# The first four steps of a fused Fourier and SoLU kernel: the next unit begun ahead of the last square, and the first sign's square ahead of the second sign's mean on ScalarE

## Chip, cores and metric

One core of a Trainium2 chip. The metric is the device time of one execution in microseconds (us). A timed value lies about 2.1 us above the span that the trace of the same execution shows, so times are compared with times and spans with spans. The experiments ran on three chips (1, 10 and 12), each kernel beside before on the same chip.

## The reference, cut to what matters

```python
def _attn_ref(x):                       # x: (8, 3136, 256)
    X = np.fft.fft(x, axis=1)
    X = np.fft.fft(X, axis=2)
    return X.real.astype(np.float32)

def _moe_ref(x, w_in, w_out, g_ln):     # x: (25088, 256), w_in: (256, 1024), w_out: (1024, 256)
    h = x @ w_in
    h_max = np.max(h, axis=-1, keepdims=True)
    e = np.exp(h - h_max)
    sm = e / (np.sum(e, axis=-1, keepdims=True) + 1e-09)
    solu = h * sm
    mu = np.mean(solu, axis=-1, keepdims=True)
    var = np.mean((solu - mu) ** 2, axis=-1, keepdims=True)
    ln = (solu - mu) / np.sqrt(var + 1e-06) * g_ln
    return (ln @ w_out).astype(np.float32)
```

## The kernel before

After a start phase that loads and narrows the weights and transforms the first pair of batches, the kernel works through 100 units of 128 rows, one unit in each step. A unit has two signs (rows k and mirrored rows), except that unit 0 has one. Names in the traces: xa and xb are loads of the next pair's input; zd is the first transform's result in DRAM, and g are its parts read back from there for the matmuls that make q; T is the table of these matmuls. A matmul of fp32 data leaves two records in the trace, a transpose one. The parts of a step that matter here:

```python
    def take2(t, ps):                       # q: second transform, PSUM to SBUF
        t.q = qpool.tile([P, KD * P], FP32, tag="q", name="q")
        nc.scalar.copy(t.q, ps)

    def spread(t):                          # r: one row of q becomes a column, 0.5 KB
        t.r = small.tile([P, 1], FP32, tag="r", name="r")
        nc.sync.dma_start(out=t.r, in_=t.q[0:1, P : 2 * P])

    def even(t, ps):                        # VectorE; waits for r
        ...
        nc.vector.scalar_tensor_tensor(out=t.ev, in0=w_mid, scalar=t.r, in1=ps, op0=ALU.mult, op1=ALU.add)

    # join: VectorE writes h = ev +- odd and its maximum; expo: ScalarE writes u = exp(h - max)

    def product(t, s, alone):               # VectorE: u = h * u and its sum; then the mean
        ...
        if alone:                           # steps 0 to 3
            nc.scalar.mul(out=t.nmean[:, s : s + 1], in_=t.usum[:, s : s + 1], mul=-1.0 / FF)
        else:
            nc.gpsimd.tensor_scalar(...)

    def square(t, s):                       # ScalarE, into h
        nc.scalar.activation(out=t.h[s], in_=t.u[s], func=ACT.Square, bias=t.nmean[:, s : s + 1],
                             accum_out=t.ssq[:, s : s + 1])

    # turn_whole (units 0 to 3): 16 TensorE transposes into four PSUM tiles ps_t, copied to uT,
    #   the first sign's two by ScalarE, the second's two by VectorE.
    #   All PSUM tiles of one bank (ps2 of q, ps_t, ps_o) share one pool of four.
    # down: 8 matmuls ps_o <- uT, Wo for each sign, four steps after the unit's own

        for i in range(len(units) + lag):   # lag = whole = 4
            ...
            if cur:
                cur.batch, cur.w = batch, i % 2
                even(cur, up(cur, 0))       # up: matmuls ps_h <- q, Wi
                odd = up(cur, 1)
            if nxt:                         # unit i + 2
                take2(nxt, transform2(pairs[nxt.p], nxt.k1))
                spread(nxt)
            if prv:
                turn_whole(prv)
            if cur:
                join(cur, odd)
            ...                             # copies ps_t to uT on VectorE
            if cur:
                expo(cur)
            ...                             # down of unit i - 4
            if cur:
                for s in cur.signs:
                    product(cur, s, i < whole)
                if i == 1:
                    weights.centre()        # VectorE: Wo = Wo - wbar, 128x2048
                for s in cur.signs:
                    square(cur, s)
                    if i >= whole:
                        turn_blocks(cur, s) # later units: blocks on VectorE, moved by DMA
            ...
            if i == 0:
                turn(first, 1, nc.sync)     # four g <- zd transfers
            ...
            if ahd:
                ahead(ahd, cur.k1)          # step 0: two xa and two xb loads of the next pair
```

Each engine runs its instructions in this program order.

## Time and profile before

| | before |
|---|---|
| time, first three runs | 1188.53, 1188.77, 1187.46 us |
| span of the profiled run (a fourth execution, timed at 1191.05 us) | 1188.9 us |
| busy share of TensorE, VectorE, ScalarE, GpSimd | 97, 76, 57, 41% |
| end of the start phase (ScalarE's copy w_mid begins) | 55.87 us |
| first ps_o, after which TensorE has no gap | 95.12 us |

### The profile page before, as it was taken

How to read it: one execution, taken by the hardware profiler on the slowest of the kernel's cores; microseconds unless marked ns; L12 is line 12 of the kernel's file. 1: busy time of each engine (PE TensorE's matmuls, PEld its weight loads, DVE VectorE, ACT ScalarE, POOL GpSimd, SP SyncE). 2: the span in 40 equal slices, each digit the busy share in tenths (PEclk: the TensorE clock that was granted, in tenths of full speed). 3: DMA queues.
4: the chain of work that ended last, by engine and by line, in shares of the span. 5: the costliest groups of instructions: out<-in, count | busy, mean ns of one | idle time of the engine just before them, and what ended most of it. 6: DMA issues, size and time to landing. Idle time of an engine off the chain costs nothing.

```text
span 1188.9 us, 15920 instructions
## 1 busy us (share of the span) xinstructions
PE 1154.8 (97%) x4720; PEld 875.7 (74%) x4720; DVE 905.3 (76%) x1234; ACT 679.6 (57%) x1411; POOL 493.0 (41%) x955
## 2 busy tenths in 40 slices
PE   2989999999999999999999999999999999999998
PEld 1556777778777777777777777777777777777787
DVE  7788777777778877787778878777786887877780
ACT  4566565656546656565555656565554555655561
POOL 3034445443545444433544453433453344333433
PEclk9999999999999999999999999999999999999999
DMA  9672877756775765654685775664684453544534
GB/s 239 191 188 47 197 180 178 202 142 156 178 170 155 189 172 153 171 145 134 166 187 158 182 177 152 159 179 121 151 200 128 112 150 98 147 111 120 142 91 118
DMA packets 458455, 185.39 MB, mean 156 GB/s; under 512 B 425751, under 2 KB 440351, under 8 KB 458369
## 3 DMA queue, kind: packets, MB, share of 16 engines
q1 hardware_dynamic: 444608, 146.22, 48.8%
q0 software_dynamic: 13760, 38.16, 11.8%
q8 instruction: 38, 0.62, 0.2%
q14 instruction: 49, 0.39, 0.1%
HBM read 44.78 MB, written 38.80 MB: 70 GB/s over the span
## 4 chain that ended last, share of the span: by engine, by line
PE 94%; DMA 2%; DVE 2%; ACT 1%; issue 1%; SPq 0%; DVEq 0%; ACTq 0%
PE ps_o L331 57%; PE ps_h L227 28%; PE ps L171 5%; PE ps L199 3%; DMA raw_in<-in_moe_w_in_dram 1%; PE wps L462 1%; DMA r<-q 1%; DVE u L259 0%; ACT h L271 0%; DVE y L123 0%; DVE h L241 0%; ACT u L251 0%; DVE xa L131 0%; DVE y L122 0%; SPq L367 0%
## 5 line engine op out<-in xcount | busy, mean ns | idle before, releaser
L331 PE MATMUL ps_o<-Wo,uT 128*128 128x256 f32 x3136 | 695.1, 380 | 0.0
L331 PEld LDWEIGHTS ps_o<-Wo,uT 128*128 128x128 f32 x3136 | 612.1, 196 | 63.0 <-issue 0.9
L227 PE MATMUL ps_h<-Wi,q 128*128 128x512 f32 x800 | 360.4, 593 | 1.7 <-DVE nmax L241 0.8
L259 DVE SCALAR_TENSOR_TENSOR u<-h,u 128x1024 f32<-128x1024 f32 x196 | 240.0, 1225 | 55.2 <-ACT u L251 28.4
L241 DVE CUSTOM_DVE_ANT_0 h<-ev,ps_h 128x1024 f32<-128x1024 f32 x196 | 231.7, 1219 | 50.5 <-PE ps_h L227 41.0
L227 PEld LDWEIGHTS ps_h<-Wi,q 128*128 128x128 f32 x800 | 151.5, 190 | 150.7 <-issue 142.3
L271 ACT ACTIVATE h<-u,nmean 128x1024 f32<-128x1024 f32 x196 | 225.0, 1149 | 55.4 <-POOL nmean L264 54.2
L264 POOL TENSOR_SCALAR nmean<-usum 128x1 f32<-128x1 f32 x189 | 76.6, 405 | 428.7 <-DVE u L259 428.3
L233 DVE SCALAR_TENSOR_TENSOR ev<-w_mid,r,ps_h 128x1024 f32<-128x1024 f32 x100 | 127.9, 1279 | 134.4 <-PE ps_h L227 124.2
L251 ACT ACTIVATE u<-h,neg 128x1024 f32<-128x1024 f32 x196 | 225.4, 1150 | 6.4
L299 DVE STREAM_TRANSPOSE v<-u 128x1024 f32<-128x1024 f32 x192 | 228.9, 1233 | 0.1
L205 ACT COPY q<-ps 128x256 f32<-128x256 f32 x100 | 37.0, 371 | 283.8 <-PE ps L199 247.6
L336 ACT ACTIVATE ot<-ps_o,rs 128x256 f32<-128x256 f32 x196 | 87.0, 461 | 60.9 <-PE ps_o L331 55.0
L343 POOL DMA_INDIRECT out_dram<-ot,idx x96 | 103.1, 1074 | 37.5 <-issue 22.8
L171 PE MATMUL ps<-y,F 98*100 98x258 f32 (+3 forms) x288 | 72.7, 390 | 23.4 <-DVE y L124 23.4
L199 PEld LDWEIGHTS ps<-T,g 128*128 128x128 f32 x400 | 60.1, 191 | 47.8 <-issue 45.9
L286 POOL TENSOR_TENSOR rs<-v,neg_half 128x2 f32<-128x2 f32 (+1 forms) x100 | 84.1, 841 | 7.8
L249 ACT ACTIVATE neg<-nmax 128x1 f32<-128x1 f32 x196 | 38.2, 195 | 62.6 <-DVE nmax L241 62.6
L283 POOL TENSOR_SCALAR v<-ssq 128x2 f32<-128x2 f32 (+1 forms) x100 | 23.7, 237 | 118.3 <-ACT h L271 118.3
L171 PEld LDWEIGHTS ps<-y,F 98*100 98x100 f32 x288 | 46.3, 180 | 35.7 <-DVE y L124 22.4
L199 PE MATMUL ps<-T,g 128*128 128x128 f32 x400 | 60.7, 275 | 0.1
L187 POOL DMA_DIRECT2D g<-zd x76 | 45.4, 610 | 30.1 <-DMA zd<-z_g 26.8
(73 smaller groups left out, 462.9 us busy)
## 6 DMA issues: line engine op xcount, KB each, us to landing
uT<-v SPq DMA_DIRECT2D x752, 128.0 KB
out_dram<-ot SPq DMA_DIRECT2D x100, 128.0 KB
g<-zd POOLq DMA_DIRECT2D x72, 160.0 KB, 5.3
xa<-in_x_dram SPq DMA_DIRECT2D x28, 392.0 KB
zd<-z SPq DMA_DIRECT2D x24, 400.0 KB
raw_in<-in_moe_w_in_dram SPq DMA_DIRECT2D x4, 512.0 KB
raw_out<-in_moe_w_out_dram SPq DMA_DIRECT2D x2, 1024.0 KB
r<-q SPq DMA_DIRECT2D x100, 0.5 KB
```

Source lines behind the costliest of these rows:

```text
L171: nc.tensor.matmul(o[..., cs], F[:, 2 * t + h, :], i[..., cs], start=first, stop=True, skip_group_check=True)
L199: nc.tensor.matmul(o, g[:, k, h * P : (h + 1) * P], table, start=(h == 0), stop=True, skip_group_check=True)
L227: nc.tensor.matmul(ps[:, fs], t.q[:, c * P : (c + 1) * P], Wi[:, c, fs], start=True, stop=True)
L233: nc.vector.scalar_tensor_tensor(out=t.ev, in0=w_mid, scalar=t.r, in1=ps, op0=ALU.mult, op1=ALU.add)
L241: nc.vector.tensor_tensor_reduce(out=t.h[s], in0=t.ev, in1=ps, scale=1.0, scalar=-3.0e38, op0=ALU.subtract if s else ALU.add, op1=ALU.max, ...
L251: nc.scalar.activation(out=t.u[s], in_=t.h[s], func=ACT.Exp, bias=t.neg[:, s : s + 1], accum_out=t.esum[:, s : s + 1])
L259: nc.vector.scalar_tensor_tensor(out=t.u[s], in0=t.h[s], scalar=1.0, in1=t.u[s], op0=ALU.mult, op1=ALU.mult, accum_out=t.usum[:, s : s + 1])
L271: nc.scalar.activation(out=t.h[s], in_=t.u[s], func=ACT.Square, bias=t.nmean[:, s : s + 1], accum_out=t.ssq[:, s : s + 1])
L299: nc.vector.transpose(out=t.batch.v[:, t.w, :, o], in_=t.u[s])
L331: nc.tensor.matmul(ps, uT[:, c, :, s], Wo[:, c, :], start=(c == 0), stop=(c == KF - 1))
L336: nc.scalar.mul(out=t.ot[s], in_=ps, mul=t.rs[:, s : s + 1])
L343: dma = nc.gpsimd.indirect_dma_start(out=out, out_offset=bass.IndirectOffsetOnAxis(ap=idx[:, i : i + 1], axis=0), in_=t.ot[s], in_offset=None)
```

## The change

The intent is to let ScalarE use its wait between the two means, and to have the next unit's q, and its transfer r, ready sooner in the first steps. The whole diff:

```diff
--- before.py
+++ after.py
@@ -604,28 +604,36 @@
         weights.load_table(1)
         lag = 4
         whole = 4
+
+        def begin(i):
+
+            cur = units[i]
+            if i % 2 == 0:
+                batches.append(Batch(i >= whole))
+            cur.batch, cur.w = batches[-1], i % 2
+            even(cur, up(cur, 0))
+            cur.odd = up(cur, 1)
+            if i + 2 < len(units):
+                nxt = units[i + 2]
+                take2(nxt, transform2(pairs[nxt.p], nxt.k1))
+                spread(nxt)
+
+        batches = []
+        begin(0)
         for i in range(len(units) + lag):
             cur = units[i] if i < len(units) else None
-            nxt = units[i + 2] if i + 2 < len(units) else None
             old = units[i - lag] if i >= lag else None
             ahd = pairs[cur.p + 1] if cur and cur.p + 1 < NP else None
             last = i >= len(units) - 2
             prv = units[i - 1] if 0 < i <= whole else None
             if i > lag:
                 store(units[i - lag - 1])
-            if cur:
-                if i % 2 == 0:
-                    batch = Batch(i >= whole)
-                cur.batch, cur.w = batch, i % 2
-                even(cur, up(cur, 0))
-                odd = up(cur, 1)
-            if nxt:
-                take2(nxt, transform2(pairs[nxt.p], nxt.k1))
-                spread(nxt)
+            if cur and i > whole:
+                begin(i)
             if prv:
                 turn_whole(prv)
             if cur:
-                join(cur, odd)
+                join(cur, cur.odd)
             if prv:
                 for o, ps in prv.wait:
                     nc.vector.tensor_copy(out=o, in_=ps)
@@ -642,19 +650,25 @@
             if cur:
                 for s in cur.signs:
                     product(cur, s, i < whole)
+                    if i < whole and s == 0:
+                        square(cur, s)
                 if i == 1:
                     weights.centre()
+                if i < whole:
+
+                    begin(i + 1)
                 for s in cur.signs:
-                    square(cur, s)
+                    if i >= whole or s:
+                        square(cur, s)
                     if i >= whole:
                         turn_blocks(cur, s)
             if old:
                 scale(old, order[0], ps_o[0])
             if cur:
                 if last:
-                    move_blocks(batch, slice(cur.w, cur.w + 1), (nc.sync, nc.gpsimd) if cur.w else (nc.sync,))
+                    move_blocks(batches[-1], slice(cur.w, cur.w + 1), (nc.sync, nc.gpsimd) if cur.w else (nc.sync,))
                 elif cur.w and i >= whole:
-                    move_blocks(batch, slice(0, 2))
+                    move_blocks(batches[-1], slice(0, 2))
                 stats(cur)
             if i == 0:
                 turn(first, 1, nc.sync)
```

No arithmetic is added or removed.

## The prediction

> **What bounds the kernel now.** I read the page's busy table first, then stretches of 5 us around the start, then the chain of work that ended last, then the timeline of the few microseconds where that chain isn't on TensorE.
>
> ```profile
> span 1188.9 us, 15920 instructions
> PE 1154.8 (97%) x4720; PEld 875.7 (74%) x4720; DVE 905.3 (76%) x1234; ACT 679.6 (57%) x1411; POOL 493.0 (41%) x955
> ```
>
> TensorE is busy for 97% of the span. A change of order on ScalarE can therefore only pay where TensorE isn't yet full. The busy table by stretches says where that is (columns: busy us of PE, weight loads, VectorE, ScalarE, GpSimd, then granted clock, DMA share, GB/s):
>
> ```profile
> 75.00:80.00 5.00, 4.01 (x18) 1.99 (x17) 4.83 (x8) 3.54 (x10) 1.16 (x3) 1.00 1.05 216
> 80.00:85.00 5.00, 3.53 (x20) 2.13 (x18) 3.41 (x6) 3.42 (x7) 1.62 (x2) 1.00 0.47 111
> 85.00:90.00 5.00, 4.02 (x12) 1.94 (x13) 4.83 (x8) 4.41 (x11) 1.12 (x3) 1.00 0.03 5
> 90.00:95.00 5.00, 2.82 (x21) 2.10 (x19) 4.79 (x8) 3.42 (x10) 2.10 (x5) 1.00 0.00 0
> 95.00:100.00 5.00, 5.00 (x18) 4.06 (x17) 4.65 (x9) 4.58 (x11) 1.14 (x4) 0.66 0.01 0
> 100.00:105.00 5.00, 5.00 (x19) 2.98 (x18) 4.04 (x4) 1.88 (x4) 3.94 (x7) 1.00 0.08 28
> ```
>
> The PE column is below 5.00 until 95 us and full afterwards; later stretches stay full, and the chain from 95.25 us to 1185 us has only TensorE pieces. So the time is "when TensorE fills up" plus a rigid remainder, and a change in the first four steps (the ones that go through TensorE transposes, roughly 58 to 95 us) is worth exactly the shift of that moment. Note the clock of 0.66 in 95 to 100. The chain before that moment:
>
> ```profile
> 73.23 1.24 ACT h L271 x2
> 74.47 0.02 issue
> 74.49 9.88 DMA r<-q
> ...
> 84.47 1.29 DVE ev L233
> ...
> 90.55 1.24 DVE u L259 x3
> ...
> 92.96 1.32 ACT h L271 x3
> 94.28 0.26 ACT q L205
> 94.55 0.04 issue
> 94.59 0.66 PE ps_t L311 x4
> 95.25 5.29 PE ps_o L331 x16
> ```
>
> Two things sit on it: the tiny transfer r (one row of q turned into a column) of unit 3, for which VectorE's ev waits, and at the end ScalarE's squares, after which come the copy q and the transposes. The timeline gives the waits in brackets and the queue of the transfers:
>
> ```profile
> 69.10 0.57 SPq L210 DMA_DIRECT2D r<-q  x1
> 70.64 2.08 SPq L187 DMA_DIRECT2D g<-zd  x4
> 72.76 0.85 SPq L109 DMA_DIRECT2D xa<-in_x_dram  x2
> 82.92 0.20 ACT L262 ACTIVATE nmean<-usum 128x1 f32<-128x1 f32 x1 [0.94 <-DVE u L259]
> 84.47 1.28 DVE L233 SCALAR_TENSOR_TENSOR ev<-w_mid,r,ps_h 128x1024 f32<-128x1024 f32 x1 [1.59 <-DMA r<-q]
> ```
>
> The r of unit 3 had its q ready at 67.7 us (ScalarE's copy at 67.38, 0.35 long), but in program order it came behind the g and xa transfers, was issued at 74.49 and landed at 84.37, behind some 1.4 MB on the same queue. VectorE sat idle 1.59 us for it. And ScalarE idled 0.94 us between the two means, while the first sign's square could have run.
>
> **What the Trainium skill says.** "PSUM — Partial Sum Buffer", Engine vs sequencer instructions: the queues of ScalarE, VectorE and GpSimd are strict FIFO, and matmuls stay in program order. The trace agrees: the first square waits at 82.92 behind the second mean, though its own mean was written 1 us before. "DMA: Bandwidth & Descriptors", Queues, rings and completion order: descriptors of one issuing queue are consumed in ring order on each DMA engine. The trace agrees: a 0.5 KB transfer took 9.88 us behind large ones. "TensorE: Matmul & The Clock Gate", Part 1, What's actually happening: the array is halved after an idle window of some 3.4 us, a free-running window; Part 4 adds that transposes don't count as busy in the same way. The trace agrees in size: from the end of the last ordinary matmul at 90.78 to the first ps_o at 95.12 only transposes ran, 4.3 us, and then the clock was 0.50 for about 3.4 us.
>
> **The change part by part.** It adds and removes no arithmetic. The comparison of instruction orders shows TensorE, VectorE and GpSimd with the same order as before. Two queues move.
>
> (1) Sync queue: the r of unit 3 now stands directly behind that of unit 2, ahead of the four g and two xa transfers. Issue about 69.7 instead of 74.49; landing I estimate at 75 to 76, right behind the r of unit 2, which the ev at 75.58 proves to be there. It is wanted at 82.80, when VectorE ends the second product of step 2. So the wait goes: ev of unit 3 starts at 82.80 instead of 84.47, a gain of **1.67 us**, all on the chain. The second xa must now wait for the second T transfer's semaphore (about 74.4), so it is issued about 1 us later; it is read only after 102 us.
>
> (2) ScalarE, steps 1 to 3: mean 0, square 0, mean 1, copy q, square 1, instead of both means, both squares, copy q. In step 1 nothing is gained: the square (pitch 1.13) just fills the wait between the means (71.6 to 72.86), the centring of Wo starts at 73.37 as before, and the next ev waits for it until 75.58. Copy q now waits for its matmuls until 74.5 and holds up the second square, whose end moves from 75.5 to about 76; h of unit 2 wants that at 78.2, so it is off the chain.
>
> Step 2: mean 0 81.77, square 0 81.88, mean 1 83.01, q 83.12 (its matmuls end at 82.25), square 1 83.37, copies uT 84.50 to 85.62. VectorE meanwhile: ev 82.80, h 84.25 and 85.40, the two copies 86.54, products 87.74 and 88.88, end 90.10. ScalarE's exponents go at 85.88 and 87.25, in time. Everything is 1.67 earlier than before, no more: in this step VectorE sets the pace.
>
> Step 3: mean 0 89.00, square 0 89.11, mean 1 90.24, q 90.35, square 1 90.60, first uT copy 91.73 to 92.35. The first ps_o needs the PSUM buffer that this copy frees, and the last four transposes, which wait for q (now at 91 instead of 94.6). Before, the first uT copy ended at 95.06 and ps_o started at 95.12; now about 92.41. Sum: **2.71 us**, of which 1.67 is from (1) and 1.04 from the square that no longer stands behind the second mean.
>
> (3) Clock: those ps_o took 5.29 us for 16 matmuls against 6.92 for 32 later, so the low clock cost 5.29 - 3.46 = **1.83 us**. The stretch without ordinary matmuls shrinks from 4.3 us (90.78 to 95.12) to 3.3 us (89.1 to 92.41). A stretch of 3.8 us (82.25 to 86.08) left the clock at 1.00 in this same run, so I expect the low clock to be gone, with a chance of 0.65, an estimate from these two stretches.
>
> Sum: 2.71 + 0.65 x 1.83 = 3.9 us off 1188.53: **1184.6 us**.
>
> **Rivals.** (a) The low clock stays: only 2.7 us come, 1185.8. For it: the window is free-running by the skill, and the three times of before spread over 1.3 us. Against: 3.3 us is under the window. If it goes in every run: 1184.0. (b) The wait for r is only replaced, by the r of unit 4 or the second g. The r of unit 4 still goes behind xa and lands at about 84.5 to 85.5, wanted at 90.03: hidden. The matmuls of unit 5's q wait for g until about 81.5 (a weight load idles 0.93 us there, put down to a ScalarE instruction long done), and copy q now stands ahead of the last square, so a late g would hold up that square; it has 0.9 us of slack. If it slips 1 to 2 us, the gain falls to 1 to 2 us: 1187. (c) The shift is given back later, because an engine behind TensorE falls short once TensorE starts earlier. Against: in step 4 VectorE would have the two block transposes done at 99.7, the next ev at once, and TensorE needs that ev only at about 103; DMA is nearly idle from 84 to 110. (d) No effect, if the r of unit 2 were itself late: 1187.5.
>
> **Range and chances.** Centre 1184.6; the two clock outcomes are 1184.0 and 1185.8; run spread is about 1.3 us. The range for 8 in 10 is 1183.0 to 1187.0. Two per cent would be 24 us, more than all idle time of TensorE after 58 us, so same: 0.99.
>
> **What would show it.** Right: no wait of ev for r in the chain; its issue before g; the two means about 1.2 us apart with the square between; first ps_o near 92.4; PE full from there; the clock of 95 to 100 near 1.00 (or the low patch moved earlier, if (a)). Wrong: VectorE waiting for r or ScalarE for the q matmuls in 82 to 84, ps_o after 94, or gaps on TensorE after 100 us.

## The result, and the profile after

The first measurement, four runs of each kernel: after 1186.47 us in the median (1185.83 to 1190.50), before 1188.65 (1187.46 to 1189.60). The ratio is 0.9989, with a 95% interval from 0.9965 to 1.0014. Ratios here are not quite the ratio of the quoted medians. The median lies in the predicted range, but the gain in the mean is 1.3 us against a forecast of 3.9, and one of the four runs took 1190.50. The profiled run of after took 1185.83.

The page of after, its head:

```profile
span 1183.7 us, 15921 instructions
PE 1151.6 (97%) x4720; PEld 873.9 (74%) x4720; DVE 904.6 (76%) x1234; ACT 679.3 (57%) x1411; POOL 494.1 (42%) x955
```

The busy table by stretches of after, with the columns as in the prediction:

```profile
80.00:85.00 5.00, 4.86 (x25) 2.79 (x24) 4.83 (x8) 4.29 (x13) 2.67 (x5) 1.00 0.27 60
85.00:90.00 5.00, 4.29 (x22) 2.72 (x22) 5.00 (x9) 4.43 (x11) 1.57 (x3) 1.00 0.00 0
90.00:95.00 5.00, 4.01 (x20) 3.48 (x20) 4.83 (x8) 4.62 (x10) 1.12 (x3) 1.00 0.01 0
95.00:100.00 5.00, 5.00 (x19) 2.98 (x18) 4.83 (x8) 3.07 (x6) 2.68 (x7) 1.00 0.00 0
```

VectorE's stretch of 80 to 85 us is filled (4.83 in place of 3.41), ScalarE's is fuller (4.29 in place of 3.42), and the clock of 95 to 100 is 1.00 in place of 0.66. (The steps lie 1.1 us earlier in this trace from the start on, as said below.) The chain that ended last in after:

```profile
72.25 2.26 DVE Wo L494
...
74.57 1.29 DVE ev L233
...
81.86 1.20 DVE ev L233
...
87.97 0.21 ACT nmean L262
88.18 0.03 issue
88.20 0.93 ACT h L271
...
89.54 0.25 ACT q L205
89.79 1.15 ACT h L271 x2
90.94 0.51 ACT uT L316
91.45 0.04 issue
91.50 3.73 PE ps_o L331 x16
```

No transfer r stands on it any more, and VectorE carries it up to the last products. At the end both squares still stand on it (88.20 and 89.79), but the first now runs beside VectorE's second product (87.85 to 89.08), so that only one comes behind that product, where there were two, and then the copy uT. The timeline of after:

```profile
67.96 1.20 SPq L210 DMA_DIRECT2D r<-q  x2
69.51 1.80 SPq L187 DMA_DIRECT2D g<-zd  x4
80.74 0.20 ACT L262 ACTIVATE nmean<-usum 128x1 f32<-128x1 f32 x1 [0.64 <-DVE u L259]
80.98 1.16 ACT L271 ACTIVATE h<-u,nmean 128x1024 f32<-128x1024 f32 x1
81.77 1.28 DVE L233 SCALAR_TENSOR_TENSOR ev<-w_mid,r,ps_h 128x1024 f32<-128x1024 f32 x1
82.13 0.19 ACT L262 ACTIVATE nmean<-usum 128x1 f32<-128x1 f32 x1
```

Two r go together ahead of g; the ev of unit 3 (81.77) has no wait in brackets; the square stands between the two means, which are 1.4 us apart, and the second one waits for nothing.

**A steadier yardstick.** The span of after is 5.2 us shorter, more than the change can be worth. Part of it lies before the change begins: the copy w_mid, which ends the start phase that is the same in both kernels, starts at 55.87 us before and 54.76 after. Over all 18 traces it starts anywhere from 53.39 to 57.44. From the w_mid copy on, the same kernel repeats itself closely: in five traces of after the first ps_o comes 36.63 to 36.74 us later, and in two of them compared step by step the next 982 us of TensorE agree within 0.01 us. So I split each span in three: to w_mid, from w_mid to the first ps_o, and from there to the end.

| kernel (trace) | w_mid at | to first ps_o | to the end | both | 16 first ps_o |
|---|---|---|---|---|---|
| before | 55.87 | 39.25 | 1093.78 | 1133.03 | 5.42, low clock |
| before again (e0) | 55.97 | 38.88 | 1094.15 | 1133.03 | 5.42, low clock |
| before, third (e10) | 54.69 | 38.42 | 1093.99 | 1132.41 | 5.42, low clock |
| after | 54.76 | 36.74 | 1092.20 | 1128.94 | 3.73 |
| after again (e1) | 56.17 | 36.63 | 1092.20 | 1128.83 | 3.73 |
| after, third (e11) | 53.39 | 36.63 | 1092.18 | 1128.81 | 3.73 |
| after, fourth (e14) | 55.51 | 36.63 | 1092.86 | 1129.49 | 3.73 |
| after, fifth (e15) | 55.43 | 36.63 | 1092.04 | 1128.67 | 3.73 |
| transfer order alone (e2) | 55.20 | 38.13 | 1093.87 | 1132.00 | 5.42, low clock |
| ScalarE order alone (e3) | 55.75 | 38.30 | 1092.25 | 1130.55 | 3.73 |
| early square alone (e4) | 56.68 | 38.49 | 1092.93 | 1131.42 | 3.73 |
| next unit begun ahead, no early square (e5) | 54.52 | 38.12 | 1091.86 | 1129.98 | 3.73 |
| before with added matmuls (e6) | 54.99 | 40.32 | 1091.99 | 1132.31 | 3.62 |
| after, held up (e7) | 55.28 | 38.94 | 1092.08 | 1131.02 | 3.73 |
| after, held up, again (e9) | 57.44 | 38.68 | 1093.68 | 1132.36 | 5.42, low clock |
| a further version (e8) | 55.99 | 34.96 | 1091.25 | 1126.21 | 3.70 |
| after, r in GpSimd's queue (e12) | 56.44 | 36.62 | 1091.54 | 1128.16 | 3.73 |
| before, r in GpSimd's queue (e13) | 56.06 | 38.17 | 1093.17 | 1131.34 | 5.41, low clock |

Differences of up to 0.8 us within the column "to the end" at the same clock lie in the tail, where the last ps_o wait up to 0.8 us in some traces and not at all in others; the five traces of after alone differ by 0.8 us there.

By this yardstick the change is worth 1132.82 - 1128.95 = 3.87 us (means of three and five traces): 2.20 before the first ps_o, 1.67 after it.

### The profile page after: what moved, and what is told of

Same layout as the page of the kernel before. It is cut to its first block, busy times and chain, and to the rows that moved or that the text cites. A ratio compares the mean times of both kernels' runs of the same rounds, so it can differ in the third digit from the quotient of the medians.

```text
span 1183.7 us, 15921 instructions
## 1 busy us (share of the span) xinstructions
PE 1151.6 (97%) x4720; PEld 873.9 (74%) x4720; DVE 904.6 (76%) x1234; ACT 679.3 (57%) x1411; POOL 494.1 (42%) x955
## 4 chain that ended last, share of the span: by engine, by line
PE 93%; DMA 3%; DVE 2%; ACT 1%; issue 1%; SPq 0%; DVEq 0%; ACTq 0%
PE ps_o L331 57%; PE ps_h L227 28%; PE ps L171 4%; PE ps L199 3%; DMA room<-in_x_dram 2%; DMA F<-in_f_tab_dram 1%; PE wps L462 1%; DVE u L259 0%; DVE h L241 0%; ACT h L271 0%; DVE y L123 0%; DVE ev L233 0%; ACT u L251 0%; DVE room L131 0%; DVE Wo L494 0%
```

## The experiments

**The two kernels again (e0, e1, e11, e14, e15).** No edit. They tell how far times of one program differ, and whether the low clock belongs to before.

> The kernel before, run against itself: what two sets of runs of one kernel differ by. Theory A (the mechanism is right, the prediction's base was the odd one: the profiled run of before had a late start and a spell of low clock that most runs don't have): ratio 1.000 within 0.001, spans spread over 1 to 2 us, and the spell of low clock near 95 us is absent (mean clock 1.000, against 0.998 in the first profile) in most runs. Rival B (the low clock belongs to the order of before and comes in every run of it): mean clock 0.998 in all its runs. In the trace, first ps_o comes 21.7 us after the centring of Wo starts, as in the first profile, in either theory.

> The changed kernel again, in more rounds. Theory A: 2.5 to 2.9 us faster than before in the median (1.67 from the transfer, 1.0 from ScalarE's order, nothing from the clock), first ps_o 19.2 us after the centring of Wo starts. Rival B: 4.2 to 4.5 us, since before has the low clock always and this one never. Rival C (the gain is partly given back later, as the single run of 1190.5 might say): 1 us or less, with gaps on TensorE after 100 us in its trace.

> The changed kernel once more, to settle the size and what the one run of 1190.5 was. From the traces so far: after takes 128.9 us plus 1000 from w_mid to the end in both its profiles, before 1132.4 to 1133.0 in three; w_mid itself comes at 54.5 to 57.4 us in thirteen traces, whichever the kernel. Theory: the gain is 3.5 to 4.1 us in the median, the runs spread over 2 to 3 us by the start alone, w_mid to end 1128.8 to 1129.3, no low clock. Rival (a second, slower way of this kernel, of which 1190.5 was one): one of six runs is again over 1189.

> The changed kernel beside the two above on the same chip, with one more trace. If the profiled run is a slow one, its trace decides: theory R, w_mid at 54 to 57 us as ever, and ev of unit 2 or 3 waiting 2 to 4 us for r; theory S, w_mid at 58 to 60 us and 1128.9 us from there. If it is a quick one: w_mid to end 1128.8 to 1129.0. Median 1185.5 to 1188.

> The changed kernel, one more trace, for the same question: a slow run, if this is one, shows either a late w_mid (theory S) or a wait for r in steps 2 and 3 (theory R); a quick one 1128.8 to 1129.0 from w_mid to the end.

| call | after: median (range) | before: median (range) | ratio (interval) |
|---|---|---|---|
| first | 1186.47 (1185.83 to 1190.50), 4 runs | 1188.65 (1187.46 to 1189.60), 4 | 0.9989 (0.9965 to 1.0014) |
| e1 | 1186.19 (1184.68 to 1187.15), 6 | 1189.46 (1187.69 to 1192.11), 11 | 0.9967 (0.9952 to 0.9981) |
| e11 | 1188.52 (1184.37 to 1189.82), 6 | 1189.84 (1188.40 to 1191.80), 8, most of an earlier call on that chip | 0.9991 (0.9975 to 1.0008) |
| e14 | 1187.12 (1186.11 to 1187.98), 5 | 1189.77 (1188.60 to 1191.91), 10 | 0.9975 (0.9961 to 0.9988) |

Before against itself (e0): 1190.24 in the median (1188.58 to 1192.40), ratio 1.0006 (0.9989 to 1.0022). So one call tells about 0.15% apart, some 1.8 us, and the change, as the traces have it, is twice that. All 22 runs of after have a mean of 1186.95 us, the 42 runs of before that were timed beside these and the other experiments 1189.66: 2.7 us. Of the 22, four took 1189.45 to 1190.50 with the clock at full (1.0); the other 18 have a mean of 1186.30, 3.4 us under before. This is what the rival of e11 expected, one run of six over 1189; there were three. Rival C of e1 has gaps on TensorE after 100 us for its sign, and none of the five traces of after has them before its tail; but none of the five is of such a slow run. Missed were also theory A's 2.5 to 2.9 us in e1 (3.3 us in the median), the 3.5 to 4.1 us in e11 (1.3 us in the median), and the 1128.8 to 1129.0 us from w_mid to the end in e14 and e15 (1129.49 and 1128.67, by their tails). What e0 expected of the clock was wrong: all three traces of before have the low clock. The record has a mean clock for other runs too. The low spell takes 0.0014 off it, so a run with 1.000 had none: 18 of 22 runs of after have 1.000, but only 2 of the 38 runs of before for which it is listed.

**The transfer order alone (e2).** In the kernel before, the g and xa transfers of step 0 move behind the r of unit 3; ScalarE is untouched.

```diff
                 spread(nxt)
+            if i == 1:
+                turn(first, 1, nc.sync)
+                ahead(pairs[1], 0)
             if prv:
                 turn_whole(prv)
...
-            if i == 0:
-                turn(first, 1, nc.sync)
-            elif i in (5, 8, 11):
+            if i in (5, 8, 11):
...
-            if ahd:
+            if ahd and i:
                 ahead(ahd, cur.k1)
```

> Part 1 alone: the r of unit 3 goes ahead of the g and xa transfers, ScalarE keeps the order of before. Theory A: first ps_o 20.1 us after the centring of Wo starts (21.75 less 1.67), time 1.7 us under before; no wait of ev for r. Rival: if the wait were only replaced by another, 0 to 0.5 us.

Measured: 1187.92 us (1186.81 to 1190.69), ratio 0.9988 (0.9972 to 1.0004). The wait for r is gone, but from w_mid to the first ps_o it is 38.13: 0.7 us less than the mean of before (38.85), not 1.67. The rest went to ScalarE. The timeline of e2 at the start of step 3:

```profile
84.75 0.08 DVE L241 DVE_READ_ACCUMULATOR2_ANT nmax<- 128x1 f32 x1
84.86 1.14 ACT L316 COPY uT<-ps_t 128x512 f32<-128x512 f32 x2
85.88 0.21 ACT L249 ACTIVATE neg<-nmax 128x1 f32<-128x1 f32 x1
```

The maximum is there at 84.83, but ScalarE, with both squares of the step before behind both means, is still at the copies uT and takes it up at 85.88. So with r early, ScalarE's order becomes the wait in its place. The low clock stays in its trace, and all six runs have a mean clock of 0.998 or 0.999.

**The ScalarE order alone (e3).** The changed kernel, with the r of unit 3 back behind g and xa.

```diff
                 take2(nxt, transform2(pairs[nxt.p], nxt.k1))
-                spread(nxt)
+                if i != 1:
+                    spread(nxt)
...
             if ahd:
                 ahead(ahd, cur.k1)
+            if i == 0:
+                spread(units[3])
```

> Part 2 alone: ScalarE in the order of after, the r of unit 3 behind the g and xa transfers as before. Theory A: the wait of ev for r stays, at 1.6 to 1.9 us; first ps_o 20.7 us after the centring of Wo starts (21.75 less 1.04), time 1.0 us under before. The two parts add up to the whole within 0.5 us. Rival: each part alone gives nothing, as either wait is enough to hold the chain.

Measured: 1187.98 us (1187.22 to 1188.83), ratio 0.9986 (0.9972 to 1.0000). From w_mid to the first ps_o 38.30, and full clock. The timeline of e3 shows the wait that stays:

```profile
84.33 1.28 DVE L233 SCALAR_TENSOR_TENSOR ev<-w_mid,r,ps_h 128x1024 f32<-128x1024 f32 x1 [1.15 <-DMA r<-q]
```

So each part alone takes 0.6 to 0.7 us off this stretch, and both together 2.2: the expectation that they add up within 0.5 us was missed. But these differences are of one trace each, and the three traces of before differ by 0.83 us. Splitting the stretch where ev of unit 3 starts tells more; the table stands after the next experiment.

**The early square alone (e4), and the next unit begun ahead without it (e5).**

```diff
# e4: the kernel before
                     product(cur, s, i < whole)
+                    if i < whole and s == 0:
+                        square(cur, s)
...
-                    square(cur, s)
+                    if i >= whole or s:
+                        square(cur, s)
# e5: the changed kernel
-                    if i < whole and s == 0:
+                    if i == 0:
                         square(cur, s)
...
-                    if i >= whole or s:
+                    if i:
                         square(cur, s)
```

> The kernel before with one thing changed: the first sign's square goes ahead of the second sign's mean on ScalarE in steps 1 to 3; copy q stays behind the last square, the transfers stay as before. Measured from the copy w_mid (the last common instruction of the start) to the first ps_o and from there to the end, before has 39.25 and 38.88, then 1093.8 and 1094.2 us; the ScalarE order of after alone has 38.30, then 1092.3. Theory A: the square is all of part 2's gain, the early q is none of it: 38.2 to 38.4, then 1092.2 to 1092.4, as the stretch without ordinary matmuls shrinks to 3.3 to 3.5 us and the clock stays full. Rival: the early copy q is what frees the last transposes, and without it first ps_o comes at 38.7 to 39.2 with the low clock after it (1093.8 to 1094.2).

> The changed kernel without the early square: the next unit is begun ahead of both squares in steps 1 to 3 (so r of unit 3 is early too), but both means come ahead of both squares. Theory A: like the transfer alone (38.13, then 1093.9 us with the low clock), since the first ps_o waits for a uT copy behind both squares either way: 38.0 to 38.3, then 1093.8 to 1094.2. Rival: the early q is worth something by itself: 37.2 to 37.7, then 1092.2.

Measured: e4 1187.44 us (1186.71 to 1190.21), ratio 0.9980 (0.9963 to 0.9996); e5 1188.96 (1186.63 to 1189.59), ratio 0.9996 (0.9980 to 1.0013). From w_mid to the first ps_o, e4 has 38.49 (e3, with the early q as well, 38.30) and e5 38.12 (e2, without the early q, 38.13). So on the way to the first ps_o the early copy q gives nothing beyond 0.2 us; what pays of "the next unit begun ahead" is the r that goes with it. What e5 expected of the clock didn't come in its trace: it was full. That did not fit a rule by the length of the stretch without ordinary matmuls, which in e5 is 4.6 us (88.07 to 92.64). But the traced run was the odd one: it has a mean clock of 1.000 and took 1186.63 us, while the other three have 0.998, 0.998 and 0.994 and took 1188.76 to 1189.59, so the low spell very likely came in them. All four runs of e4 have 1.000. So it is the early square, and not the early r, that keeps the low spell away.

The stretch from w_mid to the first ps_o, split at the start of ev of unit 3:

| kernel (trace) | w_mid to ev, us | ev to first ps_o, us |
|---|---|---|
| before, e0, e10 | 28.60, 28.24, 27.76 | 10.65 in each |
| after and its repeats (five) | 27.01, and 26.90 to 26.91 in four | 9.72 or 9.73 |
| r early, both means ahead of the squares (e2, e5, e13) | 26.93, 26.94, 26.93 | 11.21, 11.18, 11.23 |
| early square, r late (e3, e4) | 28.57, 28.59 | 9.73, 9.89 |

An early r brings ev forward by 1.27 us in the mean, but ScalarE's old order then gives 0.56 of it back behind ev. The early square is worth 0.93 us behind ev in e3 (0.76 in e4) though r is late; that e3 and e4 as wholes gain only 0.4 to 0.6 is because their r landed as late as in the first trace of before. So the square pays by itself, and the r pays in full only with it: 1.27 + 0.93 = 2.20.

**What lowers the clock (e6, e7, e9, e10).** In e6 four ordinary matmuls are added to before in the stretch of transposes; e7 delays the first ps_o of after by five small ScalarE copies; e9 is the program of e7 and e10 that of before, for other phases of the clock's window.

```diff
# e6: turn_whole of the kernel before
                 ps = ps_m.tile([P, n, P], FP32, tag="m", name="ps_t")
+                if t is units[3] and s and not half:
+                    for _ in range(4):
+                        nc.tensor.matmul(ps, ident, Wo[:, 0:2, :], start=True, stop=True)
# e7 and e9: the changed kernel
+            if i == whole:
+                scrap = fpool.tile([P, D], FP32, tag="ot", name="scrap", bufs=6)
+                for _ in range(5):
+                    nc.scalar.copy(scrap, w_mid[:, 0:D])
             if prv:
                 turn_whole(prv)
```

> The kernel before with four ordinary 128x128x512 matmuls added, 1.7 us in all, whose results are overwritten, in the stretch of transposes before the first ps_o (into a PSUM tile whose transposes come next). It tests what sets the low clock. Theory A: TensorE lowers its clock because that stretch holds only transposes for over about 3.9 us; with ordinary matmuls in it the 16 first ps_o take 3.5 to 3.8 us instead of 5.3, mean clock 1.000, first ps_o at 38.9 to 39.3 as before, then 1092.2 to 1092.5 to the end: 1.6 us faster than before although it does more work. Rival (a free-running window or the order decides): clock low as before, 1093.8 to 1094.2.

> The changed kernel with five small ScalarE copies (about 0.25 us each) ahead of the uT copies of step 4, so that the first ps_o comes about 1.25 us later. Theory A: the stretch without ordinary matmuls grows from 3.4 to about 4.7 us, so the low clock returns: first ps_o at 37.9 to 38.1 after w_mid, then 1093.8 to 1094.2 to the end, 2.9 us slower than after for 1.25 us of delay. Rival (the order of after has no low clock whatever its timing): 38.0, then 1092.2.

> The same program as the held-up one, for another phase of the clock's window. In ten traces so far the low clock came exactly where TensorE, transposes included, was busy for less than 1.5 us of one free-running window of 3.413 us (1.38, 1.38 and 1.46 before the three low spells; 1.62 the least without one). This kernel has an idle gap of 3.04 us, so most phases give a window under 1.5 us and then low clock right at that window's end; only a phase that splits the gap about in half (as in its first run: 2.17 and 1.62) gives none. Theory: low exactly if the windows of this trace say so. Rival (the order of after never has it, whatever the gap): none again, though a window is under 1.4 us.

> The kernel before, a third profile, for another phase. It has two idle gaps of 2.0 us, 8.9 us apart. Theory (a window with less than about 1.5 us busy, transposes counted, lowers the clock for the next one): a low spell right after such a window, after the first gap or after the second; full clock only if both gaps are split by a window's end. Rival (the low clock comes with this order at this place): low right at the first ps_o again, whatever the windows.

e6 measured 1190.24 us (1189.42 to 1191.73), ratio 1.0009 (0.9993 to 1.0026). The added matmuls were larger than I had reckoned, 3.6 us and not 1.7 (the timeline has them as eight records of some 0.45 us), and held up the last transposes, so the first ps_o came 1.5 us later (40.32). In its trace the clock stayed full and the 16 ps_o took 3.62 us, which gives the 1.8 us back; the sum is no gain. e7 measured 1188.85 (1188.41 to 1189.53), ratio 0.9995 (0.9979 to 1.0012): the five copies took 2.1 us and not 1.25, TensorE stood still for 3.05 us, and in its trace the clock stayed full. My theory A for e7 fell. But e9, the very same program, had the low spell, and so very likely had the other three runs of e7 (mean clock 0.994, 0.998 and 0.998) and one or two of e6 (0.998 and 0.999). The timeline of e7, then of e9:

```profile
94.22 3.73 PE L331 MATMUL ps_o<-Wo,uT 128*128 128x256 f32 x16 [3.05 <-ACT uT L316]
```

```profile
96.12 5.42 PE L331 MATMUL ps_o<-Wo,uT 128*128 128x256 f32 x16 [3.05 <-ACT uT L316]
```

Same wait, other clock. The trace's clock records explain it. Each low spell lasts 3.413 us, and the time from the first full-clock record to the low spell is a whole number of such windows (58.027 us is 17 of them before), so they tell where the windows begin in each trace. I added up TensorE's busy time in each window (ends of matmuls are modelled, so the sums are approximate), with and without the transposes:

```
trace   window, us         ordinary    with transposes   clock in the next window
before  91.95 to 95.37     0.25        1.38              low
e0      91.64 to 95.06     0.21        1.38              low
e10     90.42 to 93.84     0.73        1.38              low
e2      90.72 to 94.13     0.80        1.46              low
e13     91.49 to 94.90     0.67        1.45              low
e9      94.13 to 97.54     1.42        1.42              low
e9      90.71 to 94.13     0.00        2.23              full
e7      89.01 to 92.43     0.00        2.02              full
e7      92.43 to 95.84     1.62        1.62              full
e5      88.51 to 91.92     0.00        1.65              full
e6      82.20 to 85.61     0.30        1.71              full
```

Between 55 and 105 us of all 18 traces, the clock is low after every window in which TensorE was busy for less than 1.5 us, transposes counted, and after no other; the least without a low spell is 1.62. The sums without transposes don't sort them: 0.00 stayed full. The rule for e9 and e10 was on record before they ran, and both kept to it, which makes it more than a fit. (The 2.17 in the expectation for e9 is 2.02 by the trace.) All six low spells lie between 1.38 and 1.46, so the limit is only known to lie between 1.46 and 1.62; and a window with little work is here always one with a long gap, so the traces don't tell whether the busy time or the gap is what counts. By this rule the order of before has the low clock because it leaves TensorE standing for 2.0 us at a time (83.66 to 85.69 and 92.56 to 94.59 in its first trace), which takes a window to 1.38 wherever it falls wholly into one; after has no gap over 1.0 us from 60 us on in the four traces other than e11, and one of 1.62 there, and no window under 1.9.

**Do the slow runs come from r (e12, e13)?** In five of the first fourteen traces the ev of unit 2 starts 0.10 us after the last landing of its r (74.47 and 74.57 in after, 75.59 and 75.69 in e0; e3, e4 and e7 too), about when the centring ends: the landing stands at the edge of the chain, and in e3 ev even waited 0.35 us for it. (The expectation below says seven, which was a miscount.) So the r of units 2 and 3 were sent through GpSimd's own queue.

```diff
-    def spread(t):
+    def spread(t, engine=nc.sync):
...
-        nc.sync.dma_start(out=t.r, in_=t.q[0:1, P : 2 * P])
+        engine.dma_start(out=t.r, in_=t.q[0:1, P : 2 * P])
...
-                spread(nxt)
+                spread(nxt, nc.gpsimd if i < 2 else nc.sync)
```

> The changed kernel, with the r of units 2 and 3 sent through GpSimd's transfer queue instead of the sync queue, where they stand behind 3.2 MB of earlier transfers; nothing else. In seven of fourteen traces the ev of unit 2 started 0.10 us after the r of unit 2 had landed, so that landing is at the edge of the chain, and a run in which it comes later would be slow. Theory R (the slow runs of after, 1189.4 to 1190.5, four of sixteen with the clock at 1.0, are runs with a late r): all runs within 2 us, none over 1188, and the median about that of after's quick runs, 1185.5. Theory S (the slow runs come from the first 55 us, which are the same in all kernels): runs of 1183 to 1190 as for after in the same call.

> The kernel before with the r of units 2 and 3 in GpSimd's queue, ScalarE's order as before. It is part 1 done in a surer way. Theory R: narrower than before (whose runs spread over 4 us in each call), no run over 1190, median 1.0 to 2.0 under before. Theory S: as wide as before. In its trace no wait of ev for r, first ps_o about 38.1 us after w_mid as for the transfer order alone.

Measured: e12 1185.87 us (1184.26 to 1187.02), ratio 0.9963 (0.9950 to 0.9975); e13 1188.56 (1186.75 to 1189.57), ratio 0.9985 (0.9972 to 0.9997). Neither has a run as slow as theory R excluded, but their runs spread over 2.8 us each, where theory R had all of e12 within 2. And after itself, beside them (e14), had no slow run either (spread 1.9 us), so the comparison doesn't decide; the question stays open. Nor is GpSimd's queue free of other transfers: in e13 the r of unit 3 stood there behind two xb loads and landed 8.2 us after its issue (72.47 to 80.66), in time for 83.00; in e12, ahead of them, it took 4.7 us.

**A version that goes further (e8).** With r off the chain, VectorE carries it, and 2.29 us of that is the centring of Wo. In e8 the centring goes to GpSimd, the r of units 2 and 3 through GpSimd's queue as in e12, and the first loads of the second pair one step later.

```diff
-            nc.vector.tensor_tensor(out=Wo, in0=Wo, in1=wbar...
+            nc.gpsimd.tensor_tensor(out=Wo, in0=Wo, in1=wbar...
...
-            if ahd:
+            if ahd and i:
+                if i == 1:
+                    ahead(ahd, 0)
                 ahead(ahd, cur.k1)
```

> A version that goes further, from after: the centring of Wo goes from VectorE (2.29 us on its chain in step 1) to GpSimd, the r of units 2 and 3 go through GpSimd's own transfer queue instead of behind the large ones of the sync queue, and the first loads of the second pair come one step later. Theory A (VectorE sets the pace up to the first ps_o, so what leaves it shortens the way): ev of unit 2 starts at once after the products of step 1, first ps_o 34.3 to 35.2 us after w_mid instead of 36.7, then 1092.2; about 2 us faster than after, 5.5 to 6 faster than before. Rivals: the r of unit 2 or the g of units 5 to 9 is then the wait in place of the centring (36 to 36.7), or GpSimd and VectorE hinder each other on the same memory and VectorE's instructions of 73 to 78 us grow from 1.2 to 2 us (36.7 or more).

Measured: 1184.07 us (1183.07 to 1184.45, 5 runs) against 1189.66 (1187.91 to 1192.33), ratio 0.9949 (0.9934 to 0.9963), and correct. The timeline of e8:

```profile
72.87 1.28 DVE L233 SCALAR_TENSOR_TENSOR ev<-w_mid,r,ps_h 128x1024 f32<-128x1024 f32 x1
73.54 4.61 POOL L494 TENSOR_TENSOR Wo<-Wo,wbar 128x2048 f32<-128x2048 f32 x1 [3.14 <-ACT wbar L493]
74.32 1.22 DVE L241 CUSTOM_DVE_ANT_0 h<-ev,ps_h 128x1024 f32<-128x1024 f32 x1 [0.18 <-PE ps_h L227]
76.21 1.22 DVE L241 CUSTOM_DVE_ANT_0 h<-ev,ps_h 128x1024 f32<-128x1024 f32 x1 [0.66 <-ACT h L271]
90.95 3.70 PE L331 MATMUL ps_o<-Wo,uT 128*128 128x256 f32 x16 [1.08 <-POOL v L284]
```

GpSimd takes twice as long for the centring, but beside the chain, and VectorE's instructions next to it keep their 1.22 us. The Trainium skill, "SBUF — State Buffer", Who interferes with whom, has it so: a VectorE instruction with at most one SBUF input doesn't contend with GpSimd, outside VectorE's two-port modes; one with two inputs does while GpSimd reads SBUF. From 73.54 to 78.15 VectorE ran only ev, h and copies, each with an input from PSUM; its next product of two SBUF tiles started at 78.61, so the other half of the rule isn't tested here. Of the 2.3 us, 1.7 arrive at the first ps_o (34.96 against 36.63); 0.66 goes to a wait for the second square, which in this version comes just too late. Three things are changed at once: the r in GpSimd's queue alone gave nothing here (36.62 in e12), the later loads were not measured alone. The end comes 0.8 to 1.6 us earlier after the first ps_o than in the five traces of after, in the tail (e12 has 0.5 to 1.3 us of this too); as these differ by 0.8 us among themselves, I don't count it.

## Why the prediction was right or wrong

- **What bounds it.** Right. TensorE has no gap from the first ps_o to its tail, in every trace, and the middle 982 us agree within 0.01 us between kernels as different as after and e8; everything gained is gained before.
- **Part 1, r ahead of the large transfers: 1.67 us.** This is the term that failed: the mechanism held, the size didn't. It was taken from one trace. Against that trace it was nearly right (ev 28.60 us after w_mid before, 27.01 after: 1.59). But the wait of ev for r is 1.59, 1.21 and 0.75 us in the three traces of before, with the same instructions, and in the means ev comes 1.27 us earlier. Alone the part gave only 0.7 us (e2), since ScalarE's order then held up the next exponent.
- **Part 2, the early square: 1.04 us.** Right: from ev of unit 3 to the first ps_o it is worth 10.65 - 9.72 = 0.93 us, in every trace of before and after. With r already early it is worth more, 1.5 us (e2 and e5 against after). That the early copy q lies off the chain was implied, and e4 and e5 show it.
- **Their sum, 2.71 us to the first ps_o.** Too high by 0.5: 38.85 - 36.65 = 2.20 in the means of three and five traces. Against the first profile alone, whose 39.25 is the slowest of the three, it is 2.5.
- **Part 3, the clock: 0.65 x 1.83 us.** The result was right, the reason wrong. The low spell is gone in all five traces of after, worth 1.67 us in the means (5.42 - 3.73 = 1.69 in the 16 ps_o themselves); it was in all three of before. But the stretch without ordinary matmuls, by which I judged, doesn't decide: e7 had 5.5 us of it at full clock. (The prediction's stretch of 3.8 us ends at a weight load; to the first ordinary matmul, at 86.18, it is 3.9.) What fits every trace is windows of 3.413 us with under 1.5 us of work, transposes counted.
- **Rival (b)**, another wait in r's place: for the r of unit 4 it was wrong, that one stays hidden. For g it is nearer than the 0.9 us of slack that I gave it. In three of the five traces of after the last g lands some 0.5 to 0.8 us before the matmuls that read it (79.51 and 80.24, 80.71 and 81.55, 80.38 and 80.89). In e15 it lands at 80.55 and they start at 80.86, the weight loads ahead of them having stood 0.68 us; the copy q lost nothing there. In e11, whose steps began earliest, they waited longer, as the timeline shows:

```profile
80.54 0.68 PE L199 MATMUL ps<-T,g 128*128 128x128 f32 x4 [1.62 <-DMA xa<-in_x_dram]
81.26 0.37 ACT L205 COPY q<-ps 128x256 f32<-128x256 f32 x1 [0.43 <-PE ps L199]
```

  The bracket names xa, of the same queue, but what these matmuls read is g, whose last landing is at 80.23. The copy q, ahead of the last square, then waited 0.43 us for them. The first ps_o still came 36.63 us after w_mid, so it cost nothing there; a g later by another microsecond might. The r of unit 2 stands at the edge too, as rival (d) had it.
- **The time.** From w_mid to the end the forecast of 3.9 us is what the traces give (3.87), but by luck: the way to the first ps_o was put 0.5 us too high (2.71 against 2.20), and the clock, by its chance of 0.65, 0.5 us too low (1.19 against 1.67). In the timed runs it is 1.3 us in the first call, 3.6 in the second, and 2.7 in the mean of all. The second step that failed is "run spread is about 1.3 us", taken from three runs: one program's runs spread over 5 us before and 6 after, the start phase alone accounts for 4 us between traces, and four of 22 runs of after are slower than its traces explain; one of these, 1190.50, is among the first four. A forecast of 3.9 us could not be confirmed by four runs of each.

**What stays open:** why those four runs took 1189.45 to 1190.50. Their clock was full, so it isn't the low spell; a start phase longer than any of the 18 traced, a late r of unit 2, or a late g would each do it. That e8, which takes both r off the queue and begins the second pair's loads later, had five runs within 1.4 us fits the last two, but proves neither. No slow run was caught in a trace.

## What to carry to other kernels

Where one engine is full from some moment on, find that moment in the trace and measure a change as the shift of it, from the last point that the two kernels have in common; the whole time hides a few microseconds in the scatter of the start. A wait that is removed can uncover another: the early r alone gave 0.7 of its 1.3 us, and the rest only with the early square. A size read from one trace holds for that trace; here the same wait was 0.75 to 1.59 us in three. A small transfer that a chain waits for should not stand in a queue behind large ones (r landed 9.9 us after its issue behind g and xa, 6.6 us ahead of them), and gaps of 2 us on TensorE cost a second time here, through its clock.

## What the Trainium skill lacked or had wrong

- "TensorE: Matmul & The Clock Gate", Part 1, What's actually happening, says that the clock drops after an idle window. The free-running window of 3.413 us is confirmed, but a window need not be idle: it dropped after windows in which TensorE was busy for 1.38 to 1.46 us, 40 to 43% of it, and stayed full at 1.62. The page gives no such threshold, and one gap of 2.0 us was enough.
- The same page, Part 4, says that transposes don't count as busy in the same way. Here windows with 0.00 us of ordinary matmuls and 1.65 to 2.23 us of fp32 transposes left the clock full (e5, e7, e9), so they count for keeping it.
- "DMA: Bandwidth & Descriptors", Queues, rings and completion order, has the ring order but no figure for what it costs a small transfer: a 0.5 KB transfer took 9.88 us behind about 1.4 MB of the same queue, 10.1 us in e3, and 6.6 us ahead of them in after.

